# Grouped-query attention with a token mixer: the probabilities are placed by plain products, and placing, turns and mixer steps stand elsewhere in the program

## The chip, the core and the metric

The kernel runs on one core of one Trainium2 chip. The core has a matrix engine (PE, with its weight loads shown as PEld), a vector engine (DVE), a scalar engine (ACT), a general engine (POOL) and a queue engine (SP), which here issues nearly all transfers; 16 DMA engines move the data. The engines run side by side and wait for each other through semaphores. The metric is the device time of one execution in microseconds (us), less is better.

## The reference

`x` is 8 rows of 512 numbers, normalised once (`xn`). Two branches are added to it: attention over a cache of 8192 positions, in which 4 query heads share a key head, and a small network over the token axis.

```python
x = A_x; xn = layernorm(x)
q = (xn @ wq).reshape(8, 1, 32, 128).transpose(0, 2, 1, 3)
k = repeat(k_cache, 4, axis=1); v = repeat(v_cache, 4, axis=1)   # caches: 8 x 8 x 8192 x 128, fp32
p = softmax(einsum("bhqd,bhkd->bhqk", q, k) * 128 ** -0.5)
attn = einsum("bhqk,bhkd->bhqd", p, v).reshape(8, 1, 4096) @ wo
h = layernorm(xn)
u = gelu(einsum("bsd,sf->bdf", h, w1) + b1)                      # 1792 hidden units
mix = einsum("bdf,fs->bds", u, w2) + b2
out = x + attn + mix
```

## The kernel before

There are 64 heads of the cache (8 rows times 8 key heads). Each has 4.2 MB of keys and as many of values, 537 MB in all, and with `wq` and `wo` 553.67 MB are read once. The heads are taken two at a time, a pair at a time: 32 pairs.

**Buffers.** The even head's keys go to `K[0]`, the odd one's to `K[1]` (tile `k`), both heads' values into one buffer `VV` (tile `v`). So a pair has three loads, all on SP in this order: the values of the pair (`load_values`, L70), the keys of the next pair's even head (`load(K[0], …)`) and of its odd head (`load(K[1], …)`, both L66). The values' load may start only when the last product of the pair before has read `VV`; a key load when the scores that read that buffer are done.

**Work of a pair**, with the names of the profile:

- `turn(k, a)`, DVE: a quarter of the keys is transposed in place in blocks of 32 by 32 (L250, four quarters for a head).
- `qk(k)`, PE: the scores of one head into the PSUM tile `s` (L256, 32 rows of the profile, since each fp32 product is two passes).
- `sm_max`, `sm_bias`, `sm_exp`: DVE takes the maximum (L262), PE spreads it over the partitions with a product (L265, "the bias product", in the tile `misc`), DVE makes the bias `nb` (L268, L269), ACT the exponential into `pr` (L276).
- `sm_place(k)`, PE: products with 0/1 matrices `perms` sort the rows of a head's probabilities into the two PSUM tiles `m` (L282), the even head into their first 64 partitions, the odd one into the last 64.
- `sm_turn(h)`, DVE: tile `m` is transposed in blocks into half `h` of `pt` (L286).
- `pv`, PE: 32 products of `pt` with the values, summed in the tile `o` (L293). The first 16 need the first half of `pt`.
- `o_pick` and `o_place`, `o_sums`, `o_norm`: the result of the pair before is picked out of `o` and divided by its sum, into `ox`.
- The mixer takes an eighth of the hidden units of one row per head: `mx_pick` (DVE copies of small operands), `mx_begin` (PE, tile `mx`, L366), `mx_steps` (ACT gelu and POOL multiply and add into `macc`, L370 to L377), `mx_end` (PE, L382, into a part of the tile `mh` named `mixed`), `y_add` (DVE adds it to `yacc`, L348).

**Order.** The code is scheduled by hand: each engine does its instructions in the order in which they are written, and waits where data or buffers are not ready. `first()` does the first pair. A loop does the next 30 pairs, each as `stage_a` (the even head) and `stage_b` (the odd head, then the products with the values). Written out after the loop come the last pair, the regrouping of `ox` into `xo` (`regroup`, L489), the projection with `wo` (L562, L572) and the output. `wo` is loaded into the two key buffers in six pieces as they come free: one half into `K[0]`, the other in five pieces into `K[1]`. In the last pair each head is placed, turned and multiplied by itself (`place1`, `turn1`, `pv1`).

Of the kernel before, what the change touches and what calls it, by code (L numbers as in the profile page):

```python
# [34 lines left out]
def attn_mixer_kernel(ctx: ExitStack, tc: tile.TileContext, x, kc, vc, wq, wo, w1, b1, w2, b2, out):  # L35
# [26 lines left out]
    def load(to, src, n, pieces=(NT,)):  # L62
        rows = src.rearrange("b h (p t) d -> (b h) p t d", p=P)[n]
        at = 0
        for w in pieces:
            nc.sync.dma_start(to[:, at:at + w, :], rows[:, at:at + w, :])  # L66
            at += w
# [114 lines left out]
    O = ps_o.tile([P, 512], F32, name="o")  # L182

    MH = ps_h.tile([P, 512], F32, name="mh")
    M = [ps_m.tile([P, 512], F32, name=f"m{k}") for k in range(2)]
    MI = ps_m.tile([P, 512], F32, name="misc")
    MX = ps_m.tile([P, 512], F32, name="mx")
    pad = const.tile([P, PAD], F32, name="pad")
# [59 lines left out]
    def turn(k, a, w=NT // 4):  # L248
        t = K[k][:, a:a + w, :].rearrange("p t d -> p (t d)")
        nc.vector.transpose(t, t)  # L250
# [17 lines left out]
        nc.vector.tensor_tensor(SQ, MI[:, :P], hmask, ALU.add)  # L268
        nc.vector.tensor_reduce(NBIAS, SQ, AX.X, ALU.min)  # L269

    def sm_exp(k, halves=True):

        to, of = PR[k], S[k]
        if halves:
            to, of = to.rearrange("p (h c) -> p c h", h=2), of.rearrange("p (c h) -> p c h", h=2)
        nc.scalar.activation(to, of, AF.Exp, bias=NBIAS, scale=SCALE, accum_out=LR[:, k:k + 1])  # L276

    def sm_place(k):
        rows = slice(k * P // 2, (k + 1) * P // 2)
        for h in range(2):  # L280
            for i in range(2):
                nc.tensor.matmul(M[h][rows, :].rearrange("p (u i c) -> p i u c", u=NU, i=2)[:, i], perms[:, k, i],  # L282
                                 PR[k][:, h * 256:(h + 1) * 256].rearrange("p (u c) -> p u c", u=NU), start=True, stop=True)

    def sm_turn(h):
        nc.vector.transpose(PT[:, h * 512:(h + 1) * 512], M[h])  # L286

# [75 lines left out]
    def mx_begin(k):  # L365
        nc.tensor.matmul(MX[:FP, :], BM[k].to_broadcast([B, FP]), hn, start=True, stop=True)  # L366
# [13 lines left out]
    def mx_end(k):  # L380
        for j in range(NB):
            nc.tensor.matmul(mixed[j * Q:(j + 1) * Q, :], BW[k], ACC[:, quarter[j]], start=True, stop=True)  # L382
# [20 lines left out]
    def stage_a(s):  # L403

        load_values(s)
        for a in range(4):
            turn(0, a * quart)
        mx_end(1)
        mx_begin(0)
        for k in range(2):  # L410
            o_sums(k)
        qk(0)
        mx_steps(0, True)
        y_add()
        q_place(s + 1, 1)
        mx_pick(1, s + 1)
        for a in range(2):
            turn(1, a * quart)
        sm_max(0)
        tc.previous_stage_wait(nc.vector.engine)  # L420
        sm_bias(True)
        sm_exp(0)

    def stage_b(s):

        load(K[0], kc, s + 2)
        sm_place(0)
        for a in range(2, 4):
            turn(1, a * quart)
        mx_end(0)  # L430
        mx_begin(1)
        qk(1)
        load(K[1], kc, s + 3)
        o_pick()
        o_place()
        mx_steps(1, True)
        q_place(s + 2, 0)
        mx_pick(0, s + 2)
        y_add()
        sm_max(1)  # L440
        sm_bias()
        sm_exp(1)
        o_norm(s - 2)
        sm_place(1)
        sm_turn(0)
        tc.previous_stage_wait(nc.vector.engine)
        pv(0, NB)
        tc.previous_stage_wait(nc.tensor.engine)
        sm_turn(1)
        pv(NB)  # L450

    def first():

        qk(0)
        load(K[0], kc, 2)
        turn(1, 0)
        sm_max(0)
        sm_bias()
        sm_exp(0)
        q_place(1, 1)  # L460
        turn(1, quart)
        sm_place(0)
        mx_table()
        mx_pick(0, 0)
        mx_begin(0)
        mx_steps(0, False)
        mx_pick(1, 1)
        nc.vector.tensor_copy(yacc, mixed)
        for a in range(2, 4):
            turn(1, a * quart)  # L470
        qk(1)
        load(K[1], kc, 3)
        sm_max(1)
        sm_bias()
        sm_exp(1)
        q_place(2, 0)
        sm_place(1)
        for h in range(2):
            sm_turn(h)
        pv()  # L480
        mx_end(0)
        mx_begin(1)
        mx_steps(1, False)
        mx_pick(0, 2)
        y_add()

    def regroup(b0, b1, copy):
        for b in range(b0, b1):
# [28 lines left out]
    y_add()  # L517
    q_place(N_IT - 1, 1)
    mx_pick(1, N_IT - 1)
    for a in range(3):  # L520
        turn(1, a * quart)
    sm_max(0)
    mx_end(0)
    mx_begin(1)
    sm_bias()
    sm_exp(0, False)
    turn(1, 3 * quart)
    qk(1)
    load_wo(1, (NW - 16, 4, 2, 1, 1))
    o_pick()  # L530
    o_place()
    o_norm(N_IT - 4)
    place1(0)
    mx_steps(1, False)
    sm_max(1)
    turn1(0)
    sm_bias()
    sm_exp(1, False)
    pv1(0, 0, NU // 2)
    place1(1)  # L540
    turn1(1)
    pv1(0, NU // 2, NU)
    regroup(0, B - 1, nc.scalar.copy)
    y_add()

    o_pick()
    pv1(1, 0, NU // 2)
    o_place1()  # L550
    o_sums(0)
    o_norm(N_IT - 2, 0, 1)
    pv1(1, NU // 2, NU)
    o_sums(1)
    o_last(1)
    mx_end(1)
    o_norm(N_IT - 1, 1, 1)
    regroup(B - 1, B, nc.vector.tensor_copy)
    y_add()
    for c in range(NW):  # L560
        g = c % NG
        nc.tensor.matmul(S[0][g * Q:(g + 1) * Q, :], xo[:, c, :], WO[c // 16][:, c % 16, :], start=(c < NG), stop=(c >= NW - NG))  # L562
# [40 lines left out]
```

## Time and profile before

| | |
|---|---|
| median of 3 runs | 1302.55 us (1301.79 to 1302.96) |
| the profiled execution | 1301.4 us, of which the span (first to last instruction) is 1299.6 |
| busy share of the span | PE 71%, DVE 63%, ACT 27%, POOL 17% |
| mean granted PE clock | 0.816 of full speed |
| DMA | 553.85 MB, mean 426 GB/s |

How to read the rows. A row of the timeline has the start (us from the span's start), the time in us, the engine, the line of the code, the operation, output<-input by tile names with shapes, the number of instructions merged into the row, and in brackets the idle time before it with what ended it. Rows of several instructions may hold gaps. A row of the chain of waits has start, time, engine, output tile and line. A row of a stretch has its bounds, its length, then busy time and count of instructions for PE, PEld, DVE, ACT and POOL, the granted PE clock, the DMA engines' busy share (packets are booked where they start, so a short stretch can exceed 1) and GB/s. A row of a costly group has busy time, mean ns of one, and the idle time before it. A row of DMA issues on the page has the count, the size and the median time from issue to landing.

### The profile page before, as it was taken

How to read it: one execution, taken by the hardware profiler on the slowest of the kernel's cores; microseconds unless marked ns; L12 is line 12 of the kernel's file. 1: busy time of each engine (PE TensorE's matmuls, PEld its weight loads, DVE VectorE, ACT ScalarE, POOL GpSimd, SP SyncE). 2: the span in 40 equal slices, each digit the busy share in tenths (PEclk: the TensorE clock that was granted, in tenths of full speed). 3: DMA queues.
4: the chain of work that ended last, by engine and by line, in shares of the span. 5: the costliest groups of instructions: out<-in, count | busy, mean ns of one | idle time of the engine just before them, and what ended most of it. 6: DMA issues, size and time to landing. Idle time of an engine off the chain costs nothing.

```text
span 1299.6 us, 15867 instructions
## 1 busy us (share of the span) xinstructions
PE 916.6 (71%) x5808; PEld 317.3 (24%) x5808; DVE 816.9 (63%) x1085; ACT 355.7 (27%) x459; POOL 216.8 (17%) x201
## 2 busy tenths in 40 slices
PE   4577777758677768676668777766676567676668
PEld 1122222222222222222222222222222222222223
DVE  4557557766557666557766557666557766656772
ACT  1233323323323223323323223223323313322321
POOL 0112112112212112112112122112112212212210
PEclk9579877877969787978877768788878878897879
DMA  9999999999999999999999999999999999999996
GB/s 405 434 390 420 419 435 434 424 444 424 421 434 423 436 442 426 423 436 436 433 436 424 445 423 423 433 440 426 443 422 436 436 449 424 436 421 435 435 436 296
DMA packets 15742, 553.85 MB, mean 426 GB/s; under 512 B 2124, under 2 KB 2156, under 8 KB 2548
## 3 DMA queue, kind: packets, MB, share of 16 engines
q1 hardware_dynamic: 15300, 553.67, 99.0%
q8 instruction: 7, 0.11, 0.0%
q10 hardware_dynamic: 400, 0.02, 0.0%
q14 instruction: 3, 0.02, 0.0%
q0 software_dynamic: 32, 0.02, 0.0%
HBM read 553.69 MB, written 0.02 MB: 426 GB/s over the span
## 4 chain that ended last, share of the span: by engine, by line
DMA 51%; PE 23%; DVE 14%; issue 11%; ACT 1%; DVEq 0%; SPq 0%; POOL 0%; ACTq 0%
DMA k<-in_A_k_cache_dram 50%; PE s L256 11%; DVE k L250 11%; PE m L282 5%; PE mx L366 2%; PE o L293 2%; DVE mr L262 1%; DMA small<-in_B_w_dram 1%; PE misc L265 1%; ACT pr L276 1%; PE mh L382 1%; PE s L562 1%; DVE sq L268 0%; DVE nb L269 0%; PE o L331 0%
## 5 line engine op out<-in xcount | busy, mean ns | idle before, releaser
L250 DVE STREAM_TRANSPOSE k<-k 128x2048 f32<-128x2048 f32 x256 | 572.9, 2284 | 163.1 <-DMA k<-in_A_k_cache_dram 162.8
L256 PE MATMUL s<-k,w 128*32 128x512 f32 x2048 | 318.5, 778 | 161.6 <-DVE k L250 95.2
L282 PE MATMUL m<-pr,perms 128*64 128x256 f32 x496 | 169.2, 501 | 128.0 <-ACT pr L276 128.0
L293 PE MATMUL o<-v,pt 128*32 128x512 f32 x1984 | 239.4, 637 | 0.2
L373 POOL TENSOR_TENSOR macc<-g,mw 112x512 f32<-112x512 f32 x64 | 66.8, 1044 | 989.9 <-ACT g L370 989.9
L370 ACT ACT_TABLE_LOAD x64 | 82.1, 1283 | 509.5 <-PE mx L366 504.6
L256 PEld LDWEIGHTS s<-k,w 128*32 128x32 f32 x2048 | 81.3, 138 | 373.3 <-issue 343.7
L276 ACT ACTIVATE pr<-s,nb 128x512 f32<-128x512 f32 x64 | 72.7, 1136 | 282.8 <-DVE nb L269 178.5
L282 PEld LDWEIGHTS m<-pr,perms 128*64 128x64 f32 x496 | 79.6, 172 | 187.3 <-ACT pr L276 139.8
L370 ACT ACTIVATE g<-mx,mw 112x512 f32<-112x512 f32 x128 | 99.5, 777 | 81.9 <-POOL macc L373 77.1
L293 PEld LDWEIGHTS o<-v,pt 128*32 128x32 f32 x1984 | 63.2, 117 | 170.3 <-issue 168.6
L286 DVE STREAM_TRANSPOSE pt<-m 128x512 f32<-128x512 f32 x62 | 44.4, 717 | 87.5 <-PE m L282 86.7
L348 DVE TENSOR_TENSOR yacc<-mh,yacc 128x128 f32<-128x128 f32 x64 | 17.5, 273 | 116.4 <-PE mh L304 114.8
L377 POOL TENSOR_TENSOR macc<-macc,g 112x512 f32<-112x512 f32 x64 | 81.7, 1276 | 5.1
L378 ACT ACT_TABLE_LOAD x64 | 82.1, 1283 | 1.1
L366 PE MATMUL mx<-hn,bm 8*112 8x512 f32 x128 | 81.3, 718 | 0.0
L265 PE MATMUL misc<-nident,mr 128*128 128x128 f32 x128 | 30.3, 319 | 64.8 <-DVE mr L262 64.8
L373 POOL TENSOR_TENSOR g<-g,mw 112x512 f32<-112x512 f32 x64 | 66.5, 1039 | 56.9 <-ACT g L370 56.9
L262 DVE TENSOR_REDUCE mr<-s 128x1 f32<-128x512 f32 x64 | 43.5, 680 | 24.8 <-PE s L256 24.8
L268 DVE TENSOR_TENSOR sq<-misc,hmask 128x128 f32<-128x128 f32 x64 | 18.7, 292 | 40.7 <-PE misc L265 40.7
L265 PEld LDWEIGHTS misc<-nident,mr 128*128 128x128 f32 x128 | 19.0, 187 | 99.8 <-DVE mr L262 65.7
L382 PE MATMUL mh<-macc,bw 112*32 112x128 f32 x512 | 28.9, 302 | 6.7 <-POOL macc L377 6.7
(113 smaller groups left out, 332.8 us busy)
## 6 DMA issues: line engine op xcount, KB each, us to landing
k<-in_A_k_cache_dram SPq DMA_DIRECT2D x63, 4096.0 KB, 22.7
v<-in_A_wq_dram SPq DMA_DIRECT2D x2, 4096.0 KB, 16.8
v<-in_A_v_cache_dram SPq DMA_DIRECT2D x2, 4096.0 KB, 28.1
k<-in_A_k_cache_dram SPq DMA_DIRECT2D x2, 2048.0 KB, 30.2
k<-in_A_wo_dram SPq DMA_DIRECT2D x1, 4096.0 KB, 24.5
k<-in_A_wo_dram SPq DMA_DIRECT2D x1, 2048.0 KB, 16.8
k<-in_A_wo_dram SPq DMA_DIRECT2D x1, 1024.0 KB, 18.8
k<-in_A_wo_dram SPq DMA_DIRECT2D x1, 512.0 KB, 19.6
```

The lines of the kernel that those rows point to most:

```text
L250: nc.vector.transpose(t, t)
L256: nc.tensor.matmul(S[k][g * Q:(g + 1) * Q, :], W[k][:, j, :], kt[:, g, :, j * Q:(j + 1) * Q], start=(j == 0), stop=(j == NB - 1))
L262: nc.vector.tensor_reduce(MR, S[k], AX.X, ALU.max)
L265: nc.tensor.matmul(MI[:, :P], MR.to_broadcast([P, P]), nident, start=True, stop=True)
L276: nc.scalar.activation(to, of, AF.Exp, bias=NBIAS, scale=SCALE, accum_out=LR[:, k:k + 1])
L282: nc.tensor.matmul(M[h][rows, :].rearrange("p (u i c) -> p i u c", u=NU, i=2)[:, i], perms[:, k, i], PR[k][:, h * 256:(h + 1) * 256].rearr ...
L293: nc.tensor.matmul(O[c * Q:(c + 1) * Q, :], PT[:, u * Q:(u + 1) * Q], VV[:, u * NG:(u + 1) * NG, :].rearrange("p t d -> p (t d)"), start=( ...
L366: nc.tensor.matmul(MX[:FP, :], BM[k].to_broadcast([B, FP]), hn, start=True, stop=True)
L370: nc.scalar.activation(G, MX[:FP, :], AF.Gelu_apprx_tanh, bias=MW[k][:, 1, j:j + 1], scale=MW[k][:, 0, j:j + 1])
L373: nc.gpsimd.tensor_tensor(G if j else ACC, G, MW[k][:, 2, j:j + 1].to_broadcast([FP, D]), ALU.mult)
L377: nc.gpsimd.tensor_add(ACC, ACC, G)
L378: nc.scalar.activation(sink, epst[:1], AF.Exp)
```

## The change

Four things are different.

1. **Placing.** `sm_exp` reads the scores and writes the probabilities in their own order; before, it wrote the odd and the even columns into two halves. `sm_place(k, i)` is one product of 512 columns into one of the two banks, two for a head; before, there were four of 256 columns, written in strips of 16. Both banks are now one tile `m`. `sm_turn(h)` reads from both banks, 16 columns at a time and every second one, and so needs all products of the pair; before, each turn read one bank.
2. **The loop.** `stage_a` does three turns of `K[1]` ahead of the maximum instead of two, and has `mx_end(0)` and `mx_begin(1)`. `stage_b` begins with the last turn and `qk(1)`; the even head's two placing products stand behind `qk(1)`, one before the odd head's bias product and one after it. `y_add` stands later.
3. **`first()`.** The copy into `yacc` and the second `mx_pick` stand behind the last turns, `mx_end(0)` and what follows it before the turns of the probabilities.
4. **The last pair.** `mx_end(0)`, `mx_begin(1)` and `regroup(0, B - 1)`, `place1(0)` and the mixer's last steps stand ahead of `qk(1)`; the products with the values are split as 4, 6 and 6 around the odd head's softmax; `mx_end(1)` and the last `y_add` come earlier.

```diff
-    def sm_exp(k, halves=True):
-        to, of = PR[k], S[k]
-        if halves:
-            to, of = to.rearrange("p (h c) -> p c h", h=2), of.rearrange("p (c h) -> p c h", h=2)
-        nc.scalar.activation(to, of, AF.Exp, bias=NBIAS, scale=SCALE, accum_out=LR[:, k:k + 1])
-    def sm_place(k):
-        rows = slice(k * P // 2, (k + 1) * P // 2)
-        for h in range(2):
-            for i in range(2):
-                nc.tensor.matmul(M[h][rows, :].rearrange("p (u i c) -> p i u c", u=NU, i=2)[:, i], perms[:, k, i],
-                                 PR[k][:, h * 256:(h + 1) * 256].rearrange("p (u c) -> p u c", u=NU), start=True, stop=True)
+    def sm_exp(k):
+        nc.scalar.activation(PR[k], S[k], AF.Exp, bias=NBIAS, scale=SCALE, accum_out=LR[:, k:k + 1])
+    def sm_place(k, i):
+        nc.tensor.matmul(M[i][k * P // 2:(k + 1) * P // 2, :], perms[:, k, i], PR[k], start=True, stop=True)
     def sm_turn(h):
-        nc.vector.transpose(PT[:, h * 512:(h + 1) * 512], M[h])
+        nc.vector.transpose(PT[:, h * 512:(h + 1) * 512].rearrange("p (u i c) -> p u i c", i=2, c=16),
+                            MM.rearrange("p i (u c h) -> p h u i c", u=NU, h=2)[:, h])
...
     def stage_a(s):
...
         mx_pick(1, s + 1)
-        for a in range(2):
+        mx_end(0)
+        mx_begin(1)
+        for a in range(3):
             turn(1, a * quart)
         sm_max(0)
```

The rest is order. In the loop, PE from `qk(0)` (tile `s_185`, keys `k_81`) over `qk(1)` (`s_186`, `k_82`) to `pv` stood before like this (`pr_165` and `pr_166` are the even and the odd head's probabilities, `m_189` and `m_190` the two banks; x4 are four products):

```order
L256 MATMUL s_185<-k_81,w_162 32x512 x16
L265 MATMUL misc<-nident,mr 128x128
L282 MATMUL m_189<-pr_165,perms 64x16x16 x2
L282 MATMUL m_190<-pr_165,perms 64x16x16 x2
L382 MATMUL mh<-macc,bw_181 32x128 x4
L366 MATMUL mx<-hn,bm_180 112x512
L256 MATMUL s_186<-k_82,w_163 32x512 x16
L304 MATMUL mh<-sel_125,ob 128x8
L265 MATMUL misc<-nident,mr 128x128
L282 MATMUL m_189<-pr_166,perms 64x16x16 x2
L282 MATMUL m_190<-pr_166,perms 64x16x16 x2
L293 MATMUL o<-v,pt 32x512 x32
```

And stands now:

```order
L257 MATMUL s_185<-k_81,w_162 32x512 x16
L378 MATMUL mh<-macc,bw_181 32x128 x4
L362 MATMUL mx<-hn,bm_180 112x512
L266 MATMUL misc<-nident,mr 128x128
L257 MATMUL s_186<-k_82,w_163 32x512 x16
L277 MATMUL m<-pr_165,perms 64x512
L266 MATMUL misc<-nident,mr 128x128
L277 MATMUL m<-pr_165,perms 64x512
L300 MATMUL mh<-sel_125,ob 128x8
L277 MATMUL m<-pr_166,perms 64x512 x2
L289 MATMUL o<-v,pt 32x512 x32
```

Between the even head's bias product and the odd head's scores nothing is left; the even head's placing stands around the odd head's bias product.

In `first()`, DVE from the second `mx_pick` on (`bm_180`, `bw_182`, `mw_184` are the second head's mixer operands, `bm_179` and the like the third's) stood so before:

```order
L354 TENSOR_TENSOR bm_180<-bhot 8x1
L356 TENSOR_TENSOR bw_182<-window 112x32
L357 COPY mw_184<-table 112x6
L468 COPY yacc<-mh 128x128
L250 STREAM_TRANSPOSE k_82<-k_82 128x2048 x2
L262 TENSOR_REDUCE mr<-s_186 128x1
L268 TENSOR_TENSOR sq<-misc,hmask 128x128
L269 TENSOR_REDUCE nb<-sq 128x1
L242 TENSOR_TENSOR w_162<-qt,imask 128x128
L286 STREAM_TRANSPOSE pt<-m_189 128x512
L286 STREAM_TRANSPOSE pt<-m_190 128x512
L354 TENSOR_TENSOR bm_179<-bhot 8x1
```

And now:

```order
L251 STREAM_TRANSPOSE k_82<-k_82 128x2048 x2
L469 COPY yacc<-mh 128x128
L350 TENSOR_TENSOR bm_180<-bhot 8x1
L352 TENSOR_TENSOR bw_182<-window 112x32
L353 COPY mw_184<-table 112x6
L243 TENSOR_TENSOR w_162<-qt,imask 128x128
L263 TENSOR_REDUCE mr<-s_186 128x1
L269 TENSOR_TENSOR sq<-misc,hmask 128x128
L270 TENSOR_REDUCE nb<-sq 128x1
L344 TENSOR_TENSOR yacc<-mh,yacc 128x128
L350 TENSOR_TENSOR bm_179<-bhot 8x1
```

The last two turns of the keys `k_82` stand ahead of the copy into `yacc`, and the third head's picks ahead of the turns of `pt`.

In the last pair, PE from the odd head's scores to the regrouping stood before like this (`m_189` receives the placed probabilities, `m_190` the odd head's sum):

```order
L256 MATMUL s_186<-k_82,w_163 32x512 x16
L304 MATMUL mh<-sel_125,ob 128x8
L323 MATMUL m_189<-pr_165,perm 128x512
L265 MATMUL misc<-nident,mr 128x128
L331 MATMUL o<-v,pt 32x512 x8
L323 MATMUL m_189<-pr_166,perm 128x512
L331 MATMUL o<-v,pt 32x512 x8
L489 MATMUL misc<-fold,ox 128x32 x7
L331 MATMUL m_190<-v,pt 32x512 x8
```

And now, from the regrouping on:

```order
L488 MATMUL misc<-fold,ox 128x32 x7
L319 MATMUL m<-pr_165,perm 128x512
L257 MATMUL s_186<-k_82,w_163 32x512 x16
L327 MATMUL o<-v,pt 32x512 x4
L266 MATMUL misc<-nident,mr 128x128
L300 MATMUL mh<-sel_125,ob 128x8
L378 MATMUL mh<-macc,bw_182 32x128 x4
L327 MATMUL o<-v,pt 32x512 x6
L319 MATMUL m<-pr_166,perm 128x512
L327 MATMUL o<-v,pt 32x512 x6
L327 MATMUL m<-v,pt 32x512 x8
```

The regrouping and the first head's placing stand ahead of the scores, and the mixer's last products ahead of most products with the values.

More of the change, by code (lines that the diff above doesn't have):

```diff
@@ L184, in attn_mixer_kernel @@
     MH = ps_h.tile([P, 512], F32, name="mh")
-    M = [ps_m.tile([P, 512], F32, name=f"m{k}") for k in range(2)]
+    MM = ps_m.tile([P, 2, 512], F32, name="m")
+    M = [MM[:, k, :] for k in range(2)]
     MI = ps_m.tile([P, 512], F32, name="misc")
@@ L426, in stage_b @@
         load(K[0], kc, s + 2)
[L427 to L431, printed above, removed]
+        turn(1, 3 * quart)
         qk(1)
         load(K[1], kc, s + 3)
+        sm_place(0, 0)
         o_pick()
-        o_place()
         mx_steps(1, True)
@@ L441, in stage_b @@
         sm_bias()
+        sm_place(0, 1)
+        o_place()
         sm_exp(1)
         o_norm(s - 2)
-        sm_place(1)
+        for i in range(2):
+            sm_place(1, i)
         sm_turn(0)
@@ L461, in first @@
         turn(1, quart)
-        sm_place(0)
+        for i in range(2):
+            sm_place(0, i)
         mx_table()
@@ L466, in first @@
         mx_steps(0, False)
-        mx_pick(1, 1)
-        nc.vector.tensor_copy(yacc, mixed)
         for a in range(2, 4):
@@ L472, in first @@
         load(K[1], kc, 3)
+        nc.vector.tensor_copy(yacc, mixed)
+        mx_pick(1, 1)
+        q_place(2, 0)
         sm_max(1)
         sm_bias()
+        mx_end(0)
         sm_exp(1)
-        q_place(2, 0)
-        sm_place(1)
+        for i in range(2):
+            sm_place(1, i)
+        y_add()
+        mx_pick(0, 2)
         for h in range(2):
@@ L480, in first @@
         pv()
-        mx_end(0)
         mx_begin(1)
         mx_steps(1, False)
-        mx_pick(0, 2)
-        y_add()
     def regroup(b0, b1, copy):
@@ L519, in attn_mixer_kernel @@
     mx_pick(1, N_IT - 1)
-    for a in range(3):
+    mx_end(0)
+    mx_begin(1)
+    for a in range(2):
         turn(1, a * quart)
     sm_max(0)
-    mx_end(0)
-    mx_begin(1)
     sm_bias()
-    sm_exp(0, False)
+    turn(1, 2 * quart)
+    sm_exp(0)
+    regroup(0, B - 1, nc.scalar.copy)
+    place1(0)
+    mx_steps(1, False)
     turn(1, 3 * quart)
@@ L529, in attn_mixer_kernel @@
     load_wo(1, (NW - 16, 4, 2, 1, 1))
+    turn1(0)
     o_pick()
+    y_add()
+    pv1(0, 0, 4)
+    sm_max(1)
+    sm_bias()
     o_place()
+    mx_end(1)
+    pv1(0, 4, 10)
+    sm_exp(1)
     o_norm(N_IT - 4)
[L533 to L539, printed above, removed]
     place1(1)
+    pv1(0, 10, NU)
     turn1(1)
-    pv1(0, NU // 2, NU)
-    regroup(0, B - 1, nc.scalar.copy)
     y_add()
+    pv1(1, 0, NU // 2)
     o_pick()
-    pv1(1, 0, NU // 2)
     o_place1()
@@ L555, in attn_mixer_kernel @@
     o_last(1)
-    mx_end(1)
     o_norm(N_IT - 1, 1, 1)
     regroup(B - 1, B, nc.vector.tensor_copy)
-    y_add()
     for c in range(NW):
```

## The prediction

> **What bounds the kernel now.** I read the page's summary first, then the DVE rows that wait for key loads, then SP's issues, then the two ends of the span.
>
> ```profile
> span 1299.6 us, 15867 instructions
> DMA  9999999999999999999999999999999999999996
> q1 hardware_dynamic: 15300, 553.67, 99.0%
> ```
>
> The 16 DMA engines are busy almost throughout. The time is that of moving 553.67 MB, plus every stretch in which the queue is empty, plus what follows the last landing. So I look for empty stretches. They show in when DVE may start turning K0, which waits for its load (first the chain of waits, where each row starts at such a landing; then DVE's timeline):
>
> ```profile
> 661.23 2.34 DVE k L250 x2
> 739.67 5.82 DVE k L250 x3
> 818.07 2.67 DVE k L250 x2
> 895.46 1.48 DVE k L250
> ```
>
> ```profile
> 43.44 2.31 DVE L250 STREAM_TRANSPOSE k<-k 128x2048 f32<-128x2048 f32 x1 [4.69 <-DMA k<-in_A_k_cache_dram]
> 155.53 6.70 DVE L250 STREAM_TRANSPOSE k<-k 128x2048 f32<-128x2048 f32 x3 [6.06 <-DMA k<-in_A_k_cache_dram]
> 622.56 8.89 DVE L250 STREAM_TRANSPOSE k<-k 128x2048 f32<-128x2048 f32 x4 [6.20 <-DMA k<-in_A_k_cache_dram]
> 778.43 8.89 DVE L250 STREAM_TRANSPOSE k<-k 128x2048 f32<-128x2048 f32 x4 [0.94 <-DMA k<-in_A_k_cache_dram]
> 1204.91 2.31 DVE L250 STREAM_TRANSPOSE k<-k 128x2048 f32<-128x2048 f32 x1 [3.93 <-DMA k<-in_A_k_cache_dram]
> ```
>
> From 895.46 to 1204.91 are eight pairs (a pair moves 16.8 MB: 8.4 of values, twice 4.2 of keys): 38.68 us each, which I take as the pair's transfer time with a full queue; a key load is a quarter, 9.67. But 661.23 to 739.67 and 739.67 to 818.07 take 78.4 for two pairs, 1.05 too long each. Over the whole, 43.44 (landing of the second key load) to 1204.91 holds 29.75 pairs, 1150.7 us at the full rate; it took 1161.5. **10.8 us are lost to an empty queue**: 5.7 up to 155.53 (2.75 pairs, 106.4, took 112.1) and 5.1 later.
>
> Which load is late? The value load, which waits until the pair's last V product has read the single value buffer:
>
> ```profile
> 82.25 0.36 SPq L70 DMA_DIRECT2D v<-in_A_v_cache_dram  x1
> 600.22 9.58 SPq L66 DMA_DIRECT2D k<-in_A_k_cache_dram  x2
> 623.91 0.33 SPq L70 DMA_DIRECT2D v<-in_A_v_cache_dram  x1
> 784.69 0.33 SPq L70 DMA_DIRECT2D v<-in_A_v_cache_dram  x1
> ```
>
> ```profile
> 82.00:83.00 1.00, 0.21 (x1) 0.00 (x0) 0.94 (x1) 0.70 (x1) 0.00 (x0) 1.00 0.00 0
> ```
>
> At 82 to 83 nothing moves (last column, GB/s). In the loop, 623.91 is 1.35 us after K0's landing and nothing is lost; 784.69 is 6.26 after it, 3.4 before K1 lands, and 1.05 are lost. Taking loss to grow one for one, a value load must be issued within 5.2 us of K0's landing.
>
> **The change, part by part.**
>
> *The loop's order.* The chain to the value load runs from K1's turns to the last V product. A slow pair of before (the first row is of another place, the first pair's scores of K1 at half clock, for their price):
>
> ```profile
> 59.19 6.47 PE L256 MATMUL s<-k,w 128*32 128x512 f32 x32 [2.85 <-DVE k L250]
> ...
> 749.38 4.50 DVE L250 STREAM_TRANSPOSE k<-k 128x2048 f32<-128x2048 f32 x2 [0.22 <-DMA k<-in_A_k_cache_dram]
> 757.22 4.50 DVE L250 STREAM_TRANSPOSE k<-k 128x2048 f32<-128x2048 f32 x2
> 758.58 3.67 PE L282 MATMUL m<-pr,perms 128*64 128x256 f32 x8 [2.04 <-ACT pr L276]
> 764.74 5.27 PE L256 MATMUL s<-k,w 128*32 128x512 f32 x32
> 773.96 2.78 PE L282 MATMUL m<-pr,perms 128*64 128x256 f32 x8 [2.09 <-ACT pr L276]
> 776.67 7.87 PE L293 MATMUL o<-v,pt 128*32 128x512 f32 x64
> ```
>
> ```profile
> 759.00:760.00 1.00, 1.00 (x4) 0.55 (x3) 1.00 (x2) 0.00 (x0) 0.00 (x0) 0.50 0.91 393
> ```
>
> K1 was turned by 761.72 (757.22 + 4.50), yet its scores began at 764.74, behind the placing and the mixer on PE, at half clock (0.50). Now those stand elsewhere. DVE turns three quarters (749.38 + 6.7 = 756.1), does the maximum, waits for the bias product, and turns the fourth from about 758.0 to 760.3. The scores start at 760.4, 4.3 earlier. With PE then idle before them I give them the 6.47 of the first row instead of 5.27, so they end at 766.9, 3.1 earlier. After them a placing product stands ahead of the bias product: two passes of 512 columns, 1.8 us at half clock by the eight of 256 in 3.67 at 758.58, half of that at full. It runs beside the 0.7 of the maximum and costs the path up to 1.0. PE then works where it idled, so the last placing and V products should be warm. Against that, the first turn reads both banks and waits for all the second half's products: before it ran beside their second half, now its 0.72 is on the path. The exponential gets shorter by 0.45, since it now writes in a row as the last pairs' did:
>
> ```profile
> L276 ACT ACTIVATE pr<-s,nb x64: 687/1142/1165, 48.9 to 1273.8; 128x512 f32<-128x512 f32 x64
> ```
>
> (ns, least, median, most: 0.69 against 1.14.) Net, the value load goes about 3 us earlier, to 3 after K0's landing: inside 5.2. **The 5.1 go.** Where K1's turns already set the scores' start nothing is gained, and such pairs lose nothing today.
>
> What waits are added? PE's mixer products now wait for POOL's sum ahead of the bias product of K0's scores, and behind them wait that product, K1's scores and, through it, DVE's fourth turn:
>
> ```profile
> 593.32 1.32 POOL L377 TENSOR_TENSOR macc<-macc,g 112x512 f32<-112x512 f32 x1
> ```
>
> POOL is done at 594.64, 5.6 before 600.22, where SP issues K0's reload behind that bias product: no wait. The maximum waits behind a third turn, up to 2.24 us, and K0's reload is issued that much later; it is issued 12.7 before the value load lands (600.22 against 622.56 − 9.67) and can spare it. On SP the order of issues is unchanged; ACT and POOL do the same steps, and `o_norm` runs beside the exponential.
>
> The costs of the placing itself: four products of 256 columns become two of 512, the same columns, priced alike. The turns read every second column of two banks, which no row shows. They lie between 0.72 (below) and 0.72 × 1.66 = 1.19, by the ratio of the scattered to the plain exponential. I take 0.72, since a turn writes in a row as before; the far end adds 0.47 to a path with 2 to spare.
>
> ```profile
> L286 DVE STREAM_TRANSPOSE pt<-m 128x512 f32<-128x512 f32 x62 | 44.4, 717 | 87.5 <-PE m L282 86.7
> ```
>
> The Trainium skill speaks against such reads: "PSUM — Partial Sum Buffer", Specifications (TRN2), gives PSUM 8-byte lines and says that a non-contiguous pattern slows matmuls significantly; a read of every second value would use half of each line. By that rule the turn could exceed my bound, and the new placing product, written in a row, could undercut mine; no row here shows either.
>
> *The first pair.*
>
> ```profile
> 54.44 0.29 DVE L468 COPY yacc<-mh 128x128 f32<-128x128 f32 x1 [3.21 <-PE mh L362]
> 54.64 4.49 DVE L250 STREAM_TRANSPOSE k<-k 128x2048 f32<-128x2048 f32 x2
> 72.66 8.30 PE L293 MATMUL o<-v,pt 128*32 128x512 f32 x64
> ```
>
> DVE's copy of `yacc` waited 3.21 for PE, and two turns stood behind it. They now stand ahead of it: done near 55.5, so the scores start when PE is free, about 55.8 instead of 59.19. `mx_end(0)` (eight passes, about 0.4) leaves the end, the exponential saves 0.45, the turn adds 0.9 with its wait. The value load (82.25, 1.3 after the last V product) comes at 79.0, or near 75 if PE, now busy without a gap, gets its full clock sooner. The queue ran dry just before 82, so the first gap closes. DVE also no longer waits for `mx_end(0)` before turning K0. The second value load gains less surely: 0 to 2.4 of its gap may stay, and I leave 0.8. **4.9 of 5.7 go.**
>
> *The last pairs.*
>
> ```profile
> 1262.36 2.30 DVE L250 STREAM_TRANSPOSE k<-k 128x2048 f32<-128x2048 f32 x1
> 1264.72 6.16 PE L256 MATMUL s<-k,w 128*32 128x512 f32 x32 [2.92 <-DVE k L250]
> 1277.91 1.75 PE L489 MATMUL misc<-fold,ox 128*128 128x32 f32 x14
> 1285.44 0.43 PE L382 MATMUL mh<-macc,bw 112*32 112x128 f32 x8
> 1287.36 6.80 PE L562 MATMUL s<-k,xo 128*32 128x512 f32 x48 [0.37 <-DVE xo L491]
> 1296.45 0.29 DVE L573 COPY yacc<-mh 128x128 f32<-128x128 f32 x1 [1.79 <-PE mh L572]
> ```
>
> ```profile
> 1258.40 14.78 SPq L79 DMA_DIRECT2D k<-in_A_wo_dram  x6
> ```
>
> ```profile
> k<-in_A_wo_dram SPq DMA_DIRECT2D x1, 4096.0 KB, 24.5
> k<-in_A_wo_dram SPq DMA_DIRECT2D x2, 256.0 KB, 19.9
> ```
>
> The issues of `wo` run from 1258.40 to 1273.18, the last about 0.43 before that end; the page gives the time from issue to landing. So the first half lands at 1258.4 + 24.5 = 1282.9, the last piece at 1272.75 + 19.9 = 1292.65. The projection started at 1287.36, when both had long been or nearly been there: the end is PE's chain, not the transfers'. From the last scores' end (1270.88) that chain took 16.4 to `xo`. The regrouping (1.75), placing and turn of the first head, half its V products (a quarter of 7.87) and `mx_end(1)` (0.43) move into stretches where PE waits; about 11.6 remain. The fourth turn ends some 0.6 later, the scores take 6.16 at half clock or some 3.4 at full, so `xo` comes at 1280.4 to 1283.1: about when `wo`'s first half lands. From there PE keeps up with the pieces; after the last landing come the last eight passes (0.3) and what stands behind them today, 1296.41 to 1299.6. End 1292.65 + 0.3 + 3.2 = 1296.15: **3.3 go** (3.45, less a little for a cold clock).
>
> **Sum.** 5.1 + 4.9 + 3.3 = 13.3. The profiled execution took 1301.4 (span 1299.6 and 1.8 around it): 1288.1. The runs' median, 1302.55, is 1.15 above it: 1289.3.
>
> **Rivals.**
>
> 1. *The loop still starves.* The placing no longer keeps PE busy between the two heads' scores. If scores, both placings and V products all fall on half clock (6.5, 3.7 and 8.3 at the rows' cold durations), the value load of the slow pair comes at 784.6, as today, and the 5.1 stay: 1294.4. For it: the row at 759 has the clock at half in the midst of such work. Against: after 760.4 PE hardly idles. The Trainium skill, "TensorE: Matmul & The Clock Gate", What's actually happening, says that one busy window of about 3.4 us frees the clock. By that rule no run behind the scores would be at half clock, and this rival would vanish. The trace is less kind: the scores at 59.19 took 6.47, with no sign of a freed clock after 3.4.
>
> 2. *The last pairs stay on PE's chain* or meet a new wait (the mixer's products on POOL's sum, ahead of V products). `xo` at 1287 again gives back the 3.3: 1292.6.
>
> 3. *Slower: the strided turn.* Nothing shows its price. The value load has about 2.2 left in slow pairs and 3.9 in fast ones (5.2 − 1.35); a first turn dearer by more than 3.9, so above 4.6, would empty the queue in all 31 pairs. At 5.6 that is 31 us: 1320. The scattered exponential, 1.66 times, speaks against it.
>
> 4. *No change:* the gaps only move, say from value loads to K0's reloads: 1302.
>
> **Chances.** Forecast 62%, its own range 1286.5 to 1291.5; rival 1 15%, rival 2 15%, rivals 3 and 4 4% each. Low 1286.5: the 0.8 and 0.15 held back, the 1.15 by which the profiled run lay below the median, and 0.7 for the reading of the rate (0.02 a pair). High 1297 takes in rivals 1 and 2, and both together (1297.7) almost. No change means within 0.2%, 2.6 us, about what these runs can tell. Faster 0.92, same 0.04, slower 0.04.
>
> **What would show it.** K0's landings 38.7 apart from 100 us on, with no zero stretch near 82; value loads within 5 us of them; in slow pairs the scores of K1 right behind the fourth turn; turns of about 0.72; the projection starting near `wo`'s first landing and ending some 3.5 behind its last. It would be wrong if 78 us per two pairs recur, if the turn shows over 1.2, or if PE at the end waits on POOL or DVE instead of `wo`.

## The result and the profile after

| | before | after |
|---|---|---|
| median of 6 runs each | 1302.17 us (1298.68 to 1306.05) | 1288.32 us (1287.07 to 1289.59) |
| ratio after to before | | 0.9893, 95% interval 0.9875 to 0.9911 |
| span of the profiled execution | 1299.6 us | 1286.3 us |
| last landing of `wo` (from the trace's DMA events) | 1292.65 us | 1281.55 us |

The change makes the kernel 1.07% faster. The span is 13.3 us shorter, which is the predicted sum. Its parts are not those of the prediction: the transfers end 11.1 earlier (10.0 were forecast), and what follows the last landing is 2.2 shorter (6.95 to 4.75; 3.3 were forecast). That the sum agrees to the tenth is chance: the two errors cancel. One run of all those below, 1528.81 us at a granted clock of 0.54 instead of about 0.8, counts in no ratio.

The chain of waits of the kernel after (start, time, engine, output, line), first and last of the rows in which DVE takes up K1 at its landing; and on DVE's timeline the same event of the first pair:

```profile
span 1286.3 us, 15395 instructions
DMA  9999999999999999999999999999999999999998
275.63 4.83 DVE k L251 x3
314.41 5.90 DVE k L251 x3
353.03 5.36 DVE k L251 x3
...
1203.97 4.88 DVE k L251 x3
```

```profile
43.63 2.31 DVE L251 STREAM_TRANSPOSE k<-k 128x2048 f32<-128x2048 f32 x1 [4.68 <-DMA k<-in_A_k_cache_dram]
```

From 43.63 to 1203.97 are 30 pairs: 38.68 each. The queue does not run empty any more; before, 29.75 pairs had taken 10.8 too much.

A pair that answers to the slow one shown of before, from PE's, DVE's and SP's timelines:

```profile
750.66 6.38 PE L257 MATMUL s<-k,w 128*32 128x512 f32 x32 [3.05 <-DVE k L251]
760.22 1.93 PE L277 MATMUL m<-pr,perms 128*64 128x512 f32 x4 [0.40 <-ACT pr L273]
762.19 1.31 DVE L281 STREAM_TRANSPOSE pt<-m 128x512 f32<-128x512 f32 x2 [1.70 <-PE m L277]
763.05 7.08 PE L289 MATMUL o<-v,pt 128*32 128x512 f32 x64 [0.90 <-DVE pt L281]
768.91 8.89 DVE L251 STREAM_TRANSPOSE k<-k 128x2048 f32<-128x2048 f32 x4 [5.41 <-DMA k<-in_A_k_cache_dram]
770.24 0.33 SPq L70 DMA_DIRECT2D v<-in_A_v_cache_dram  x1
```

The value load is issued 1.3 us after K0's landing (768.91), where it was 6.26. Three stretches of this pair (bounds, length, busy time of PE, PEld, DVE, ACT, POOL, then PE's granted clock, DMA share, GB/s): K1's scores, placing with softmax, and the V products.

```profile
750.66:757.04 6.38, 6.38 (x33) 1.45 (x34) 2.60 (x8) 2.93 (x4) 3.38 (x3) 0.56 0.86 375
756.98:762.15 5.17, 4.77 (x16) 1.44 (x12) 1.84 (x6) 0.78 (x2) 0.00 (x0) 1.00 1.03 444
763.05:770.13 7.08, 7.08 (x72) 2.68 (x72) 1.67 (x2) 0.00 (x0) 0.00 (x0) 1.00 1.03 444
```

Only the scores pay for the half clock now. The placing and the V products behind them, in this and in all pairs of the loop, run at 1.00.

The last pair, PE and DVE:

```profile
1242.80 4.50 DVE L251 STREAM_TRANSPOSE k<-k 128x2048 f32<-128x2048 f32 x2
1248.57 0.69 DVE L263 TENSOR_REDUCE mr<-s 128x1 f32<-128x512 f32 x1 [1.26 <-PE s L257]
1250.73 4.49 DVE L251 STREAM_TRANSPOSE k<-k 128x2048 f32<-128x2048 f32 x2
1255.28 4.96 PE L257 MATMUL s<-k,w 128*32 128x512 f32 x32 [0.20 <-DVE k L251]
1273.80 7.05 PE L563 MATMUL s<-k,xo 128*32 128x512 f32 x48 [0.30 <-DVE xo L490]
1283.14 0.29 DVE L574 COPY yacc<-mh 128x128 f32<-128x128 f32 x1 [1.79 <-PE mh L573]
```

The projection still waits for `xo` and not for `wo`, whose first half landed at 1271.71.

### The profile page after: what moved, and what is told of

The parts are those of the page before. It is cut to its first block, busy times and chain, and to the rows that moved or that the text cites. A ratio compares the mean times of both kernels' runs of the same rounds, so it can differ in the third digit from the quotient of the medians.

```text
span 1286.3 us, 15395 instructions
## 1 busy us (share of the span) xinstructions
PE 895.5 (70%) x5560; PEld 288.8 (22%) x5560; DVE 826.9 (64%) x1085; ACT 332.5 (26%) x459; POOL 217.9 (17%) x201
## 4 chain that ended last, share of the span: by engine, by line
DMA 54%; DVE 23%; PE 18%; issue 5%; ACT 0%; SPq 0%; DVEq 0%; POOL 0%; ACTq 0%
DMA k<-in_A_k_cache_dram 53%; DVE k L251 20%; PE s L257 15%; DVE mr L263 2%; PE misc L266 1%; DMA small<-in_B_w_dram 1%; DVE sq L269 1%; PE o L289 1%; PE s L563 1%; PE o L327 0%; PE m L327 0%; PE mx L362 0%; DVE nb L270 0%; PE m L277 0%; SPq L66 0%
## 5 line engine op out<-in xcount | busy, mean ns | idle before, releaser
L257 PE MATMUL s<-k,w 128*32 128x512 f32 x2048 | 371.4, 892 | 285.3 <-DVE k L251 186.3
L289 PE MATMUL o<-v,pt 128*32 128x512 f32 x1984 | 219.3, 593 | 27.8 <-DVE pt L281 27.8
L257 PEld LDWEIGHTS s<-k,w 128*32 128x32 f32 x2048 | 90.1, 156 | 516.0 <-issue 456.5
L273 ACT ACTIVATE pr<-s,nb 128x512 f32<-128x512 f32 x64 | 44.0, 687 | 439.6 <-DVE nb L270 282.8
L277 PE MATMUL m<-pr,perms 128*64 128x512 f32 x248 | 127.7, 618 | 16.3 <-ACT pr L273 16.3
L289 PEld LDWEIGHTS o<-v,pt 128*32 128x32 f32 x1984 | 73.6, 110 | 172.7 <-issue 171.0
L281 DVE STREAM_TRANSPOSE pt<-m 128x512 f32<-128x512 f32 x62 | 40.7, 695 | 53.5 <-PE m L277 53.5
L362 PE MATMUL mx<-hn,bm 8*112 8x512 f32 x128 | 72.7, 647 | 0.0
L277 PEld LDWEIGHTS m<-pr,perms 128*64 128x64 f32 x248 | 26.6, 136 | 68.8 <-issue 45.7
L297 DVE TENSOR_TENSOR ob<-ob 128x128 f32<-128x128 f32 x32 | 30.9, 967 | 1.1
```

The lines of the kernel that those rows point to most:

```text
L257: nc.tensor.matmul(S[k][g * Q:(g + 1) * Q, :], W[k][:, j, :], kt[:, g, :, j * Q:(j + 1) * Q], start=(j == 0), stop=(j == NB - 1))
L273: nc.scalar.activation(PR[k], S[k], AF.Exp, bias=NBIAS, scale=SCALE, accum_out=LR[:, k:k + 1])
L277: nc.tensor.matmul(M[i][k * P // 2:(k + 1) * P // 2, :], perms[:, k, i], PR[k], start=True, stop=True)
L289: nc.tensor.matmul(O[c * Q:(c + 1) * Q, :], PT[:, u * Q:(u + 1) * Q], VV[:, u * NG:(u + 1) * NG, :].rearrange("p t d -> p (t d)"), start=( ...
```

## The experiments

All are timed beside the kernel before. Its median was 1302.40 beside the four single parts, 1301.62 beside the longer chains, the fillers and the last pair taken further, and 1299.61 beside the held-back value loads and the old first pair; its single runs lay between 1294.7 and 1308.2. The changed kernel was not timed again beside these runs. Where a run is compared with its 1288.32, the ratio to the kernel before is the second measure.

**1. The parts, each alone.** Four kernels are the kernel before with one of the four differences: the first pair's order, the loop's order, the last pair's order, the form of placing. The one place where old and new had to be fitted together is the loop's order with the old placing, which places the even head's two banks apart:

```diff
-    def sm_place(k):
+    def sm_place(k, hs=(0, 1)):
...
-        for h in range(2):
+        for h in hs:
...
+        sm_place(0, (0,))      # behind qk(1)
...
+        sm_place(0, (1,))      # behind the odd head's bias product
```

> The kernel before with only the new order of the first pair (the copy into yacc and the picks behind the last turns, the mixer's end ahead of the exponential); placing, loop and last pair as before. Theory A (the terms are separate, each closes its own gap): the first value load is issued near 75 to 79 instead of 82.25, the gap of 3.8 us near 104 goes, the one of 1.7 near 145 goes or stays, and the loop's later gaps stay: faster by 3.8 to 5.7, 1296.5 to 1298.5. Theory B (the loop's late pairs are only the echo of the bad start; with the queue full from the start no pair is late): faster by 9 to 11, near 1292.

> The kernel before with only the loop's new order (third turn ahead of the maximum, mixer products behind the even head's scores, the odd head's scores right behind the fourth turn, the even head's placing around the odd head's bias product); the placing keeps its old form of four products and a scattered exponential, first pair and last pair as before. Theory A: the late pairs of the loop go, and with them the gap near 145, which lies in the loop's first pair; the gap near 104 stays: faster by 5 to 7, 1295 to 1297. Theory C (it is the form of placing and exponential that shortens the chain): faster by less than 2.6.

> The kernel before with only the new order of the last pair; its exponential was a plain one there already. Theory A: the last transfer lands when it did, and the end comes 4.8 instead of 6.95 behind it: faster by 2 to 2.4, 1300. A rival (the projection waits for the transfers, which come no earlier than before, so the shorter chain buys nothing): no change, 1302.

> The kernel before with only the new form of placing: two products of 512 columns a head, a plain exponential, turns that read both banks; every step in its old place. Theory A: the exponential's 0.45 us, gained for each head, is given back by the first turn's wait for all products; the late pairs stay late: no change within 2.6 us, 1300 to 1304. Theory C (the form carries the gain in the loop): faster by 4 to 6.

| alone | median | ratio to before (95%) | last landing | end behind it | lost in the first three pairs | lost in the next 26 |
|---|---|---|---|---|---|---|
| (before) | 1302.40 | | 1292.65 | 7.0 | 5.6 | 5.2 |
| first pair | 1297.96 | 0.9961 (0.9942 to 0.9980) | 1290.51 | 8.1 | 2.7 | 5.1 |
| loop's order | 1293.43 | 0.9938 (0.9917 to 0.9959) | 1284.26 | 7.0 | 2.9 | 0.0 |
| last pair | 1301.00 | 0.9982 (0.9964 to 0.9999) | 1294.42 | 6.3 | 7.9 | 5.1 |
| placing | 1292.96 | 0.9926 (0.9906 to 0.9946) | 1286.11 | 6.0 | 4.3 | 0.5 |
| all (the change) | 1288.32 | 0.9893 (0.9875 to 0.9911) | 1281.55 | 4.8 | -0.3 | 0.0 |

The last four columns are of one profiled execution each; "lost" is the time between landings of K0, from the DMA events, above 38.68 a pair (the first three pairs count from the landing at 72 us).

The four medians add up to 24 us; together the parts bring 14. Theory B falls: with a better start the loop's late pairs stay (5.1 lost, as before). Theory A's times hold for the first and the last pair within the noise. The profiled executions bear it out only in part: with the first pair's order alone 2.7 of the 5.6 stay lost, and with the last pair's the end is 6.3 behind the last landing and not 4.8. It fails for the placing, for which it expected nothing and Theory C 4 to 6. Placing alone and the loop's order alone each bring 9, more than any theory gave them: each frees the loop of its 5 us of late pairs, and the loop's order takes the loss of the loop's first pair too (3.0 us there before, 0.1 with it). The chain of waits of the kernel with the placing alone, rows in which DVE starts at a landing of K0:

```profile
347.86 3.26 DVE k L251 x2
425.26 3.94 DVE k L251 x2
...
1198.89 1.68 DVE k L251
```

347.86 to 1198.89 are 22 pairs at 38.68, none late, with every step in its old place. The chain from K1's landing to the value load shows why. Measured pair by pair, without the first three, it is 28.1 to 35.3 us in the kernel before, 28.8 to 31.7 with the new placing, 28.7 to 29.9 with the new order and 29.3 to 30.5 with both. Loads become late from about 34 to 35 on, and those of before missed what is needed by 1.2 us or less. So 1.2 are enough, and the 3.6 to 5.4 that each part takes off the longest chain are mostly to spare. Both together are no better than either: with the new placing the chain of the new order is even 0.6 longer. That this is the first turn's wait for all products is likely, not shown. With the placing alone K1's scores take 3.64 in every settled pair, the time at full clock, where those of the late pairs of before take 5.0 to 5.3. So part of what the placing takes off the longest chain, 1.4 us or more, is PE's clock, against 0.9 for the two shorter exponentials.

**2. The first pair, taken out of the change.**

```diff
-        nc.vector.tensor_copy(yacc, mixed)
-        mx_pick(1, 1)
+        mx_pick(1, 1)
+        nc.vector.tensor_copy(yacc, mixed)
         for a in range(2, 4):
             turn(1, a * quart)
...                                # and the rest of first() as before
```

> The changed kernel with the first pair in its old order (the new form of placing kept). Theory A: the loop stays free of late pairs, and the first two value loads lose what they lost in the runs with only the loop's order or only the new placing, 3 to 5: 1291 to 1293. A rival (with the new placing the old order is early enough): 1288.

1290.47, ratio 0.9929 (0.9903 to 0.9956) to the kernel before: 2.2 above the whole change by the medians, 4.7 by the ratios, whose intervals overlap. So in company the first pair's order is worth something between 2 and 5, and these runs can't say more. The trace shows why. The first value load is issued at 78.05 (changed kernel 74.81, before 82.25), and the last transfer lands 1.7 later. But that load moves by as much with no change of code at all. The first pair of before stands unchanged in four kernels. Its load is issued at 82.25, 82.05, 81.44 and 78.38 (before, with filler products, last pair's order alone, loop's order alone). PE's granted clock changes only every 3.41 us, and in these executions a step of that grid falls 61.5, 61.3, 60.6 and 60.1 us after the span's start. The first pair of the change does the same: 77.72 and 77.76 with a step at 61.6 and 61.7 (six more turns, last pair taken further), 74.88 and 74.81 at 59.6 and 59.9 (twelve more turns, the changed kernel). In the run here, with a step at 61.8, the old order's 78.05 is only 0.3 behind the new order at a like place of the grid. The new placing alone takes the load to 80.33.

**3. How late may a value load be?** First the whole chain was made longer, by turning the probabilities' first half six or twelve times more:

```diff
-        sm_turn(0)
+        for _ in range(7):         # 13 in the second kernel
+            sm_turn(0)
```

> The changed kernel with six more copies of the first turn of the probabilities in each pair of the loop (each about 0.63 us on DVE, right ahead of the products with the values): the chain to the value load grows by 3.8 us, from 29.3 to 30.5 up to 33.1 to 34.3. Theory A (a value load costs nothing until it is issued less than about 2 us before the next keys' load begins to land; the changed kernel has 6.4 at least, so 4.3 to spare): no change against the changed kernel's 1288.3, within 1.3. A rival (the chain itself is the period, or a later value load always costs): 3.8 a pair, 1400.

> The same with twelve more copies: the chain grows by 7.5 us to about 37 to 38. Theory A: past the 4.3 to spare the queue runs empty in every pair, by 2.5 to 3.7 us each in 30 pairs: 1360 to 1400. If later loads cost nothing at all (the queue never was the bound): 1288.

1340.69 (ratio 1.0305, 1.028 to 1.0331) and 1467.81 (1.1282, 1.1247 to 1.1317). Both expectations failed: 52 us where nothing was expected, and 179 us where 72 to 112 were. The six turns delayed the products by 4.5 (PE's wait is 5.41 instead of 0.90) and not by 3.8. While they ran PE was idle, and then (PE's and DVE's timeline, and PE's clock in the stretch of the V products):

```profile
750.57 5.82 DVE L281 STREAM_TRANSPOSE pt<-m 128x512 f32<-128x512 f32 x8 [1.70 <-PE m L277]
755.94 9.72 PE L289 MATMUL o<-v,pt 128*32 128x512 f32 x64 [5.41 <-DVE pt L281]
```

```profile
755.94:765.66 9.72, 9.72 (x72) 2.88 (x72) 8.88 (x5) 0.00 (x0) 0.00 (x0) 0.72 1.00 432
```

The V products took 9.72 instead of 7.08, their clock was 0.72 instead of 1.00, and K0's scores, and with them the next pair's steps, began up to 2 us later behind them. The chain grew from about 30 us to between 37.3 and 40.6. So this pair of kernels did not vary the issue time alone. The next three do: only SP waits longer, through a copy by DVE of one column of the value buffer, put behind the second, third or fourth turn of K0.

```diff
-        load_values(s)
-        for a in range(4):
+        for a in range(2):         # 3, 4
+            turn(0, a * quart)
+        nc.vector.tensor_copy(hold, VV[:, 0, :1])
+        load_values(s)
+        for a in range(2, 4):      # the turns that are left
             turn(0, a * quart)
```

> The changed kernel with the value load held back alone, in every pair of the loop: DVE copies one column of the value buffer behind the second turn of K0, and the load waits for that copy. No engine's work moves. The load is issued about 4.6 us behind K0's landing, some 3.6 ahead of the first landings of K1. Theory A (a load issued 2 us or more ahead of those costs nothing; the prediction's own bound is 5.2 behind K0's landing): no change against the changed kernel's 1288.3, within 1.5. A rival, after the run with six more turns that was 52 us slower (every us by which the value load comes later costs about one): 2 to 4 a pair, 1350 to 1400.

> The same behind the third turn: issued about 6.8 us behind K0's landing, 1.3 ahead of the first landings of K1. Theory A: 0.7 a pair are lost by the 2 us of lead, 1.6 by the prediction's bound of 5.2: 20 to 48 slower than the changed kernel, 1308 to 1336. If it does not slow at all, the bound is wrong.

> The same behind the fourth turn: issued about 9 us behind K0's landing, when K1 lands. Theory A: 2.2 more a pair than behind the third turn, one for one: 2.9 to 3.8 a pair, 85 to 115 slower than the changed kernel, 1373 to 1403.

Medians 1293.31 (ratio 0.9946, 0.9921 to 0.9971), 1325.18 (1.0180, 1.0145 to 1.0215) and 1350.55 (1.0391, 1.0356 to 1.0426): 5, 37 and 62 above the changed kernel (7, 37 and 65 by the ratios). The first expectation, nothing within 1.5, failed too: a load 3.3 us ahead still costs a little. Two value loads in a row of the one behind the fourth turn, with K0's landings on DVE:

```profile
439.60 8.89 DVE L252 STREAM_TRANSPOSE k<-k 128x2048 f32<-128x2048 f32 x4 [8.27 <-DMA k<-in_A_k_cache_dram]
480.44 8.89 DVE L252 STREAM_TRANSPOSE k<-k 128x2048 f32<-128x2048 f32 x4 [8.49 <-DMA k<-in_A_k_cache_dram]
```

```profile
448.67 0.33 SPq L70 DMA_DIRECT2D v<-in_A_v_cache_dram  x1
489.51 0.33 SPq L70 DMA_DIRECT2D v<-in_A_v_cache_dram  x1
```

9.1 behind K0's landing, and 40.8 from load to load instead of 38.7. Over 24 pairs of each kernel, with the lead of a value load over the first landings of K1 read from the DMA events:

| kernel | mean lead, us | pair, us | loss a pair |
|---|---|---|---|
| changed | 7.0 | 38.68 | 0.00 |
| load behind two turns | 3.3 | 38.80 | 0.12 |
| two filler products (below) | 1.7 | 39.25 | 0.57 |
| load behind three turns | 1.0 | 39.88 | 1.20 |
| six more turns | 0.6 | 40.11 | 1.43 |
| load behind four turns | 0.0 | 40.66 | 1.98 |
| twelve more turns | -3.8 | 44.37 | 5.69 |

Below a lead of about 2 us the loss is 2 us less the lead, one for one, whatever makes the load late; the two runs with more turns, which failed their expectations, lie on the same line. At 3.3 a loss of 0.12 is left; with the placing alone, whose settled leads are 4.6 to 7.0, there is none. These are means: with the fillers the pairs alternate between leads of 0.8 and 2.6, and only the first kind loses time. The largest case of the three lost less than expected (62, not 85 to 115), since the estimate took the 16 engines' landings as far apart as in the changed kernel (1.8 us on average). With a queue that runs empty in each pair they are 0.7 apart, so K1's first landing comes later and the lead there is 0 and not below.

**4. Filler products in the kernel before**, to keep PE's clock up:

```diff
         for a in range(4):
             turn(0, a * quart)
+        for i in range(2):         # the result is not used
+            nc.tensor.matmul(S[1], ident, K[0][:, quart + 4 * i:quart + 4 * i + 4, :].rearrange("p t d -> p (t d)"),
+                             start=True, stop=True)
         mx_end(1)
```

> The kernel before with two filler products a pair (128 columns of weights, 512 columns of K0's second quarter, into the odd head's free scores tile, behind the second turn of K0, where PE waits for the other two turns). They compute nothing that is used. Theory D (the late pairs of before are those whose scores and placing fall on PE's half clock; whatever keeps the clock up or shifts it takes the lateness away): K0's scores at 3.7 to 5 instead of up to 6.5 us, few or no late pairs: faster by 4 to 9, 1293 to 1298. Theory A alone (only the order or the form of the steps helps, and PE has two products more): no change or slower, 1302 to 1306.

1312.4 (ratio 1.0081, 1.0055 to 1.0107): slower. On PE's timeline stand the scores of K0, the placing and the scores of K1 of one pair:

```profile
521.64 3.64 PE L256 MATMUL s<-k,w 128*32 128x512 f32 x32
...
530.10 3.68 PE L282 MATMUL m<-pr,perms 128*64 128x256 f32 x8 [2.04 <-ACT pr L276]
...
536.27 5.03 PE L256 MATMUL s<-k,w 128*32 128x512 f32 x32
```

K0's scores did come down to 3.64 us, as theory D had it, but they started later (0.2 to 2.4 behind K1's landing, where the kernel before has 0.6 ahead of it), and the clock was back at half for the placing and most of K1's scores. Raising the clock at one place does not help where the time is spent two waits later.

**5. The last pair taken further.**

```diff
+    regroup(0, B - 1, nc.scalar.copy)   # and two filler products, behind K0's turns
     mx_end(1)
     mx_begin(0)
...
     sm_max(0)
-    sm_bias()
+    nc.tensor.matmul(MI[:, :P], MR.to_broadcast([P, P]), nident, start=True, stop=True)
     turn(1, 2 * quart)
+    nc.vector.tensor_tensor(SQ, MI[:, :P], hmask, ALU.add)
+    nc.vector.tensor_reduce(NBIAS, SQ, AX.X, ALU.min)
     sm_exp(0)
-    regroup(0, B - 1, nc.scalar.copy)
     place1(0)
```

> The changed kernel with the last pair taken further: the regrouping of the first seven rows and two filler products stand ahead of the last even head's scores, where PE waits for the turns, and the third turn of the odd head stands in the wait for the bias product. Theory A (after the change the end is still PE's chain, 1.25 us above what the transfers allow): the projection starts at the landing of the first half of wo, and the span ends 3.5 instead of 4.75 behind the last landing: about 1287, faster than the changed kernel by 0.7 to 1.25. A rival (the clock of the projection sets the end): it ends 4.5 or more behind the last landing, 1288.

1288.88 (ratio 0.9902, 0.988 to 0.9924): nothing gained, as the rival had it. The profiled execution, the slowest of the six (1291.25), ends 6.0 behind its last landing. The idle time that it meant to fill is not free:

```profile
1236.08 0.52 PE L492 MATMUL misc<-fold,ox 128*128 128x32 f32 x3
1240.40 2.56 PE L492 MATMUL misc<-fold,ox 128*128 128x32 f32 x11 [3.80 <-issue]
1242.77 3.61 PE L401 MATMUL s<-k,ident 128*128 128x512 f32 x4
1248.24 3.64 PE L257 MATMUL s<-k,w 128*32 128x512 f32 x32
```

PE stands still for 3.80 us behind the loop's end, with no semaphore to wait for, whichever product is next (in the changed kernel it stands 3.90 ahead of `mx_end`). In both gaps, and not once in the loop between 110 and 1230 us, the trace's DMA packets have one of 16 KB in queue q8, kind "instruction" (1238.20 to 1239.17 here, 1236.04 to 1237.00 in the changed kernel). So PE probably waits for its next code; no run tested it. The added products therefore moved K0's scores from 9.0 to 13.4 us behind K0's landing (1232.99 in the changed kernel, 1234.88 here).

## Why the prediction was right, point by point

**The bound.** Right: the time was that of a full queue plus its gaps plus the end, and in this execution the gaps are gone.

**The loop, 5.1.** The size is right and so are the steps to the scores: they start 10.9 behind K1's landing instead of 15.4, 4.5 earlier (4.3 forecast), and take 6.38 (6.47). What follows was thought to lose a little and gained 1.5 (scores' end to value load 14.7, now 13.2), because placing and V products are at full clock throughout. What fell is the attribution. The prediction gave the 5.1 to the order and priced the placing at nothing. The order is enough, as it said, but the experiments show that the new form of placing is by itself enough too. How exactly the new form takes the late pairs away, through its 0.45 twice a pair or through the clock that falls differently, was not separated.

**The bound of 5.2 behind K0's landing.** Nearly right: at 4.7 the loss is 0.12 a pair, and at 6.9 it is 1.20 where the bound gives 1.7. The better measure is the lead over the next landings, 2 us.

**The first pair, 4.9.** In this execution all 5.7 went, so the 0.8 held back was not needed: the loads came at 74.81 (75 to 79 forecast) and 115.62, with no loss behind either. But the order is not the cause of all of it, and part is luck (experiment 2). In the execution of experiment 5, whose first pair is that of the changed kernel, the load came at 77.76 and about 2 us were lost.

**The last pair, 3.3.** The mechanism holds, the size is off: 2.2. The step that failed is "the fourth turn ends some 0.6 later". It ended 12.5 behind K1's landing instead of 10.8, 1.7 later: the third turn now stands behind a maximum that waits 1.26 for K0's scores (1248.57). So `xo` came 31.0 behind K1's landing, not 26.5 to 29.2. (The scores at full clock, put at some 3.4, take 3.64 wherever these traces have them at 1.00; here they took 4.96.) The 2.2 is no accident of one execution. In the six with the new last pair and no turns added to the loop the end comes 3.7 to 6.5 behind the last landing, on average 5.1, and in the five with the old one 6.0 to 8.1, on average 7.1. The rest is PE's clock in the projection. Where it starts early, the end comes as forecast: in the kernel with the old first pair it starts 0.9 behind the landing of `wo`'s first half, waits for the last piece (0.21), and the span ends 3.7 behind that:

```profile
1274.29 6.66 PE L563 MATMUL s<-k,xo 128*32 128x512 f32 x48 [0.30 <-DVE xo L490]
1283.29 0.43 PE L573 MATMUL mh<-k,xo 128*32 128x128 f32 x8 [0.21 <-DMA k<-in_A_wo_dram]
```

With the last pair's order alone it starts 2.5 behind and takes 8.17 instead of 6.66, and the end comes 6.3 behind the last landing.

**The new forms.** Turn, exponential and placing on the page of the kernel after (busy us, mean ns of one):

```profile
L281 DVE STREAM_TRANSPOSE pt<-m 128x512 f32<-128x512 f32 x62 | 40.7, 695 | 53.5 <-PE m L277 53.5
L273 ACT ACTIVATE pr<-s,nb 128x512 f32<-128x512 f32 x64 | 44.0, 687 | 439.6 <-DVE nb L270 282.8
```

The turn that reads every second column of two banks takes 0.70, no more than the plain one (0.72): the value taken, at the low end of the range. The rule of the Trainium skill, "PSUM — Partial Sum Buffer", Specifications (TRN2), that was weighed against it does not show in DVE's reads here; the page's words are of matmuls, and the prediction stretched them to these reads. Placing costs the same per column, as priced: four passes of 512 columns take 1.93 at full clock (760.22 above), and before, where the clock was full, eight of 256 in strips took 1.94:

```profile
329.09 1.94 PE L282 MATMUL m<-pr,perms 128*64 128x256 f32 x8 [1.95 <-ACT pr L276]
```

So what the same rule would make dearer in the old placing does not show either.

**The rivals.** The loop does not starve on a half clock: behind the scores the clock is 1.00. This is what the rule of the Trainium skill, "TensorE: Matmul & The Clock Gate", What's actually happening, gave, against the prediction's reading of the 6.47. The page also calls the window of 3413 ns free-running, so that a run of products that starts inside one waits for the next to end. The trace agrees: the clock is granted at 64.9, 5.7 us after those scores began at 59.19 and one full step of the grid after 61.5, so the 6.47 is no contradiction. Rival 2 came true by a third: 1.1 of the 3.3 stayed. Rivals 3 and 4 fall with the turn at 0.70 and with transfers that end 11.1 earlier.

## What to carry to other kernels

Where a queue of transfers bounds the time, find for each load how far ahead of the queue's end it is issued: here about 2 us were needed, less cost one for one, and from 4.6 on more brought nothing. Near such a limit the parts of a change do not add, since any of them may carry all the load to the safe side, so price them by the margin that is missing (1.2 us) and not by what each saves. And a wait ahead of a long run of products can cost more than its length: with 5.4 us of idle time ahead of them the V products ran at a clock of 0.72 and took 2.6 us longer.

## What the runs showed of the hardware

*The clock changes only on a grid, and where the grid falls moves the work.* In the kernel before the granted clock changes only at steps of 3.413 us (five stretches between its changes in the slow pair):

```profile
754.43:757.84 3.41, 1.22 (x10) 0.30 (x2) 1.85 (x4) 0.48 (x1) 0.00 (x0) 1.00 0.85 365
757.84:768.08 10.24, 9.50 (x34) 3.11 (x38) 5.68 (x9) 2.74 (x4) 0.96 (x1) 0.50 0.92 400
768.08:774.91 6.83, 3.66 (x29) 1.59 (x22) 1.94 (x7) 3.40 (x5) 2.38 (x3) 1.00 1.05 456
774.91:778.32 3.41, 3.41 (x13) 1.00 (x15) 1.43 (x2) 0.00 (x0) 0.00 (x0) 0.50 1.00 432
778.32:788.56 10.24, 9.15 (x86) 3.09 (x82) 9.91 (x10) 2.06 (x2) 0.46 (x1) 1.00 0.95 387
```

All the traces of this case show such steps. Experiment 2 has what their place does: one and the same first pair issues its value load up to 3.9 us earlier or later.

Some loops that are late keep step with the grid. The 78.4 that two pairs took there is near 23 steps (78.51); with the filler products two pairs take 78.5 as well, with twelve more turns 88.7 (26 steps, 88.75), with six more turns four pairs take 160.4 (47 steps, 160.43). Not all do: the first late pairs of before take 78.7 for two, and with the load behind four turns a pair takes 40.66, 11.9 steps. In the changed kernel the transfers set the pace, 116.05 for three pairs, and this happens to be 34 steps (116.05), so its chain repeats every third pair: 30.5, 29.9, 29.3. That the runs of before scatter (1294.7 to 1308.2, the changed kernel's 1287.1 to 1289.6) because the grid falls differently in each is likely; no experiment moved the grid by itself.

*The two us ahead of an empty queue* stand ahead of the data. With twelve more turns the queue is empty when the value load is issued, at 392.24 in one pair (the last column is GB/s):

```profile
388.60:392.24 3.64, 3.64 (x44) 1.08 (x35) 3.44 (x2) 0.00 (x0) 0.00 (x0) 1.00 0.00 0
392.24:393.18 0.94, 0.94 (x6) 0.27 (x2) 0.00 (x0) 0.00 (x0) 0.00 (x0) 1.00 0.00 0
```

By the trace's DMA packets the 16 engines start their first ones 0.95 to 2.05 us behind the issue in the settled pairs, on average 1.2, and these take 3.06 us where the next ones take 2.42. That makes 1.8 of the 2. The fixed cost of about 2.0 us that the Trainium skill gives in "DMA: Bandwidth & Descriptors", Anatomy of one DMA — SWDGE (gpsimd) path, is another thing, though the size agrees: these loads are issued by SP, and that page speaks of another path and puts most of the cost behind the last byte.
